# Linear attention in pairs of batches, with 64x64 quarters of the matmul array

## The chip, the cores and the metric

The kernel runs on one core of one Trainium2 chip. The metric is the device time of one execution in microseconds. The core has a matmul engine (PE, with its weight loads shown as PEld), VectorE (DVE), ScalarE (ACT), GpSimd (POOL) and SyncE (SP), which here only issues loads; 16 DMA engines serve all transfers between HBM and the on-chip memory of 128 partitions. Matmul results go to PSUM[...].

## The reference

Two parts follow each other: a linear attention with a norm, and a mixture of experts in which each token goes to one expert.

```python
# q, k, v: (8 batches, 8 heads, 576 tokens, 64) fp32
kv  = einsum('bhsd,bhse->bhde', k, v)        # 64 x 64 per batch and head
out = einsum('bhsd,bhde->bhse', q, kv)
rms = sqrt(mean(out * out, axis=-1) + 1e-6)
x   = (out / rms * g_norm)                   # then (4608 tokens, 512)

logits     = x @ w_gate                      # 8 experts
expert_idx = argmax(logits, axis=1)
gate_w     = softmax(logits)[expert_idx]
for e in range(8):                           # w1: 512 x 1024, w2: 1024 x 512
    ye = relu(x[mask_e] @ w1[e]) @ w2[e]
    out[mask_e] = gate_w * ye
```

## The kernel before

The attention stage works on 36 tiles of 128 tokens with all 8 heads (512 values a token). A batch has 576 tokens, that is four and a half tiles. Of each batch, 512 tokens lie with four tokens in each of 128 partitions; the 64 tokens left over ("rem") of two batches share a tile, 64 partitions each. So a pair of batches has nine tiles: four, four, and one of the remainders.

```python
def load_qkv(src, b):
    t = PA.tile([128, 8, 256], F32, tag="ld", bufs=6, name="ld")
    nc.sync.dma_start(
        t, src[b, :, 0:512, :].rearrange("h (p j) d -> p h (j d)", j=4)
    )
    return t

def load_rem(t, src, b, eng):
    bb = b % 2
    eng.dma_start(
        t[64 * bb:64 * bb + 64, :, :], src[b, :, 512:576, :].transpose([1, 0, 2])
    )
```

One piece of a main load is thus four tokens of one head, 4 x 64 x 4 B = 1 KB, and one of a remainder 256 B. The sums k^T v of a batch are made for two heads at a time, in two column halves of the array:

```python
def kv_mm(b, i):
    # ...
    for j in range(5):
        for hh in range(2):
            h = 2 * i + hh
            if j < 4:
                lhs = kb[:, h, 64 * j:64 * j + 64]
                rhs = vb[:, h, 64 * j:64 * j + 64]
            else:
                lhs = kr[r0:r0 + 64, h, :]
                rhs = vr[r0:r0 + 64, h, :]
            nc.tensor.matmul(
                kvp[64 * hh:64 * hh + 64, i, :], lhs, rhs,
                start=(j == 0), stop=(j == 4),
            )
```

They are copied to a block-diagonal matrix of two heads (`kvs`, zero elsewhere), with 16 more columns that hold kv times the gate's weights. One tile of q is transposed (`x_qt`), copied by ScalarE (`x_qs`) and multiplied with these matrices, 128 rows by 144 columns:

```python
def x_mm(s):
    P, r, b = split(s)
    if r < 8:
        parts = [(slice(0, 128), kvs_bufs[b % 4])]
    else:
        parts = [(slice(0, 64), kvs_bufs[(2 * P) % 4]),
                 (slice(64, 128), kvs_bufs[(2 * P + 1) % 4])]
    op = PSA.tile([128, 2, 512], F32, tag="op", bufs=2, name="op")
    for i in range(4):
        c0 = (i % 2) * 144
        for c, kvs in parts:
            nc.tensor.matmul(
                op[c, i // 2, c0:c0 + 144], qts[s][:, i, c], kvs[:, i, :],
                start=True, stop=True,
            )
    return op
```

`x_norm` squares `op` on ScalarE (`sq`), sums on VectorE (`ms`), makes the factor with ln and exp on ScalarE (`lnt`, `rinv`), and scales on VectorE: the gate's columns (`lr`) and the rows (`xg`). After four or five tiles a `Route` finds the expert of each token and its rank there; GpSimd then writes each tile's rows to a scratch in HBM by an indirect DMA (`xs_scratch`). The order of one step is fixed by hand:

```python
for s in range(36):
    op = x_mm(s)
    for fn in mid[s]: fn()
    if s + 2 < 36: qt = x_qt(s + 2)
    rest = x_norm(s, op)
    if s + 2 < 36: x_qs(s + 2, qt)
    for fn in late[s]: fn()
    rest()
    for fn in last[s]: fn()
```

`load_batch(b + 2)` and the copies `heads` of q (GpSimd, from the loaded tile to one with the heads side by side) are put into `last`, `kv_mm` into `late`. The loads of the first two experts' weights follow those of the last batches in the same queue. Then, in the second stage, each expert's rows are gathered, transposed (`xp`), multiplied by w1 (`hp`), put through relu (`ht`), multiplied by w2 (`yp`), scaled (`ys`) and scattered to the output.

Of the kernel before, what the change touches and what calls it, by code (L numbers as in the profile page):

```python
# [21 lines left out]
def _bc(ap: bass.AP, insert_pos: int, count: int) -> bass.AP:  # L22
    dims = [list(d) for d in ap.ap]
    dims.insert(insert_pos, [0, count])
    return bass.AP(tensor=ap.tensor, offset=ap.offset, ap=dims)
# [3 lines left out]
def kernel(  # L29
# [11 lines left out]
    nc = tc.nc  # L41
# [30 lines left out]
    for P in range(4):  # L72
        for bb in range(2):
            for j in range(4):
                c32[:, o + 9 * P + 4 * bb + j] = (2 * P + bb) * S + 4 * ar + j
        c32[:64, o + 9 * P + 8] = 2 * P * S + 512 + ar[:64]
        c32[64:, o + 9 * P + 8] = (2 * P + 1) * S + 512 + ar[:64]
# [29 lines left out]
    wg = P_const.tile([128, 4, 8], F32, tag="wg")  # L107
    g2 = P_const.tile([128, 1], F32, tag="g2")
    gw = P_const.tile([128, 4, 2, 8], F32, tag="gw")
# [20 lines left out]
    class Weights:  # L130
# [19 lines left out]
        def stage_in(self, pool, tag, bufs):  # L150

            self.s1, self.s2 = [], []
            for dst, src in ((self.s1, moe_w1), (self.s2, moe_w2)):
                rows = src[self.e, :, :].rearrange("o (t p) f -> p (o t) f", p=128)
                n = rows.shape[1] // 2
                for m in range(2):
                    t = pool.tile([128, n, rows.shape[2]], F32, tag=tag, bufs=bufs, name="ws")
                    nc.sync.dma_start(t, rows[:, n * m:n * m + n, :])
                    dst.extend([t[:, kk, :] for kk in range(n)])

        def half1(self, eng, kk):
            if kk == 0:
                self.w1 = P_w.tile([128, 4, F], F16, tag="w1e", bufs=2, name="w1e")
            st = self.s1[kk] if isinstance(self.s1, list) else self.s1[:, kk, :]
            if eng is nc.scalar:
                eng.activation(self.w1[:, kk, :], st, ACTF.Copy, scale=g2)
            else:
                eng.tensor_scalar(  # L168
                    self.w1[:, kk, :], st, g2, 1.0, op0=ALU.mult, op1=ALU.mult,
                )  # L170

        def half2(self, kk):
            if kk == 0:
                self.w2 = P_w.tile([128, 8, D], F16, tag="w2e", bufs=2, name="w2e")
            if isinstance(self.s2, list):
                for m in (2 * kk, 2 * kk + 1):
                    nc.scalar.copy(self.w2[:, m, :], self.s2[m])
            else:
                nc.scalar.copy(  # L179
                    self.w2[:, 2 * kk:2 * kk + 2, :], self.s2[:, 2 * kk:2 * kk + 2, :]  # L180
                )
# [6 lines left out]
    with (  # L188
# [4 lines left out]
        kvs_bufs = []  # L193
        for n in range(4):
            t = PA.tile([128, 4, 144], F32, tag=f"kvs{n}", name=f"kvs{n}")
            kvs_bufs.append(t)

        def load_qkv(src, b):
            t = PA.tile([128, 8, 256], F32, tag="ld", bufs=6, name="ld")
            nc.sync.dma_start(  # L200
                t, src[b, :, 0:512, :].rearrange("h (p j) d -> p h (j d)", j=4)
            )
            return t

        def rem_tile(tag):
            return PA.tile([128, 8, 64], F32, tag=tag, bufs=2, name=tag)

        def load_rem(t, src, b, eng):
            bb = b % 2
            eng.dma_start(  # L210
                t[64 * bb:64 * bb + 64, :, :], src[b, :, 512:576, :].transpose([1, 0, 2])
            )

        ld, rem, qp, kvst = {}, {}, {}, {}
        srcs = {"k": k, "v": v, "q": q}

        def load_first():

            for n in "kvq":
                rem[n, 0] = rem_tile(n + "r")  # L220
                if n != "q":
                    ld[n, 0] = PA.tile([128, 8, 256], F32, tag="ld", bufs=6, name="ld")
            for n, eng in (("k", nc.sync), ("v", nc.scalar)):
                load_rem(rem[n, 0], srcs[n], 0, eng)
                for hs in (slice(0, 4), slice(4, 8)):
                    eng.dma_start(
                        ld[n, 0][:, hs, :],
                        srcs[n][0, hs, 0:512, :].rearrange("h (p j) d -> p h (j d)", j=4),
                    )
            nc.sync.dma_start(cf, c_f32.ap())  # L230
            ld["q", 0] = load_qkv(q, 0)
            nc.scalar.dma_start(wg, moe_w_gate.rearrange("(t p) j -> p t j", p=128))
            nc.scalar.dma_start(g2[0:64, :], g_norm.unsqueeze(1))
            nc.scalar.dma_start(g2[64:128, :], g_norm.unsqueeze(1))
            for n in "kv":
                ld[n, 1] = load_qkv(srcs[n], 1)
                load_rem(rem[n, 0], srcs[n], 1, nc.sync)
            ld["q", 1] = load_qkv(q, 1)
            for b in range(2):
                load_rem(rem["q", 0], q, b, nc.sync)  # L240
            nc.sync.dma_start(ch, c_f16.ap())

        def load_batch(b):
            for n in "kvq":
                ld[n, b] = load_qkv(srcs[n], b)
                if b % 2 == 0:
                    rem[n, b // 2] = rem_tile(n + "r")
                    for bb in range(2):
                        load_rem(rem[n, b // 2], srcs[n], b + bb, nc.sync)

        def heads(b, j):

            if j == 0:
                qp[b] = PA.tile([128, 4, 8, 64], F32, tag="qp", bufs=2, name="qp")
            tv = ld["q", b].rearrange("p h (j d) -> p h j d", j=4)
            nc.gpsimd.tensor_copy(qp[b][:, j, :, :], tv[:, :, j, :])  # L256


        def kv_mm(b, i):
            if i == 0:  # L260
                kvst[b] = PSA.tile([128, 4, 64], F32, tag="kvp", bufs=1, name="kvp")
            kvp = kvst[b]
            kb, vb = ld["k", b], ld["v", b]
            kr, vr = rem["k", b // 2], rem["v", b // 2]
            r0 = 64 * (b % 2)
            for j in range(5):
                for hh in range(2):
                    h = 2 * i + hh
                    if j < 4:
                        lhs = kb[:, h, 64 * j:64 * j + 64]  # L270
                        rhs = vb[:, h, 64 * j:64 * j + 64]
                    else:
                        lhs = kr[r0:r0 + 64, h, :]
                        rhs = vr[r0:r0 + 64, h, :]
                    nc.tensor.matmul(  # L275
                        kvp[64 * hh:64 * hh + 64, i, :], lhs, rhs,
                        start=(j == 0), stop=(j == 4),
                    )

        def kv_copy(b):  # L280
            kvp, kvs = kvst[b], kvs_bufs[b % 4]
            for hh in range(2):
                ps = slice(64 * hh, 64 * hh + 64)
                nc.vector.tensor_copy(kvs[ps, :, 64 * hh:64 * hh + 64], kvp[ps, :, :])

        def kv_t(b):
            kvs = kvs_bufs[b % 4]
            kvtp = PSA.tile([128, 4, 128], F32, tag="misc", bufs=1, name="kvtp")
# [534 lines left out]
```

## Time and profile before

The median of three runs is 307.33 us (306.12 the lowest). The profiled execution has a span of 303.6 us.

| group | count | busy us | mean ns of one |
|---|---|---|---|
| PE `op` = q times kv, 128x144 (and the remainders' form) | 320 records | 45.5 | 301 |
| PE `kvp` = k^T v, 128x64 | 512 records | 22.0 | 228 |
| DVE `ms`, sums of squares | 36 | 24.4 | 679 |
| DVE `xg`, scaled rows | 36 | 24.5 | 681 |
| ACT `sq` / `qts` | 36 / 36 | 21.4 / 20.9 | 593 / 582 |
| POOL scatter to the scratch | 36 | 35.4 | 983 |

The page gives for each engine its busy share in the span and in 40 slices of 7.6 us, in tenths; the rows DMA and GB/s say how busy the 16 DMA engines were and what they moved. A matmul of fp32 shows as two records. Records of the PE overlap in time, so the distance between starts says more than the duration of one. The stages can be told apart by the groups: the first `op` starts at 21.3 us, the last tile's rows are scaled at 131.4 us, and the experts' products run from 145 us to the end. A table of stretches gives busy times, the granted clock of the PE, the DMA share and GB/s for any window.

### The profile page before, as it was taken

To read this page: it belongs to the slowest core of one execution; us is meant where nothing else is said; L and a number is where in the kernel's file an instruction comes from. 1 tells how busy PE (TensorE), PEld (TensorE's weight loads), DVE (VectorE), ACT (ScalarE), POOL (GpSimd) and SP (SyncE) were. 2 spreads that over 40 slices of the span, in tenths; PEclk is the share of its full clock that TensorE was granted. 3 is DMA by queue.
4 is the path that set the end of the run, shared out by engine and by line. 5 is a ranking of instruction groups with operands and counts; after the bars stand their busy time and mean duration, and the time that the engine had idled before them with its cause. 6 is when DMAs were issued, how large, how long until landed. Compare 5 with 4: busy or idle time off the path is not lost.

```text
span 303.6 us, 6229 instructions
## 1 busy us (share of the span) xinstructions
PE 275.5 (91%) x2349; PEld 189.7 (62%) x2349; DVE 164.0 (54%) x431; ACT 159.2 (52%) x342; POOL 153.2 (50%) x205
## 2 busy tenths in 40 slices
PE   8697989899989987647979999999999999999993
PEld 3376877788878886513644756647566574665652
DVE  0024576768778777781237946445464553556140
ACT  1024556556564665488530674737657365672831
POOL 9332016438636764665762576457365663215052
PEclk9799999999999999869999999999999999999998
DMA  6999999999999999922894299979799898968421
GB/s 188 341 284 279 243 279 349 301 276 351 333 299 315 386 401 405 367 105 71 268 364 171 86 367 305 399 220 393 282 346 347 266 388 276 353 279 270 167 101 66
DMA packets 59790, 85.66 MB, mean 282 GB/s; under 512 B 16493, under 2 KB 41326, under 8 KB 59760
## 3 DMA queue, kind: packets, MB, share of 16 engines
q1 hardware_dynamic: 50512, 65.10, 67.7%
q0 software_dynamic: 6976, 18.96, 17.2%
q10 hardware_dynamic: 2272, 1.20, 1.5%
q8 instruction: 19, 0.31, 0.4%
q14 instruction: 11, 0.09, 0.1%
HBM read 71.71 MB, written 15.50 MB: 287 GB/s over the span
## 4 chain that ended last, share of the span: by engine, by line
PE 30%; issue 10%; DMA 9%; POOL 4%; POOLq 1%
PE yp L691 14%; PE hp L677 14%; DMA out_dram<-ys,idx 7%; POOL out_dram L699 2%; DMA xe<-xs_scratch,rowi 2%; PE xp L658 2%; POOL xe L630 2%; POOLq L818 0%; POOL xs_scratch L450 0%; POOLq L699 0%; POOLq L630 0%; POOLq L783 0%
## 5 line engine op out<-in xcount | busy, mean ns | idle before, releaser
L684 ACT ACTIVATE ht<-hp 128x320 f16<-128x320 f32 (+1 forms) x136 | 57.9, 428 | 70.0 <-PE hp L677 58.6
L677 PE MATMUL hp<-xt,w1e 128*128 128x320 f16 (+1 forms) x544 | 79.3, 294 | 0.1
L699 POOL DMA_INDIRECT out_dram<-ys,idx x41 | 42.6, 1038 | 65.7 <-DVE ys L696 56.6
L691 PE MATMUL yp<-w2e,ht 128*128 128x512 f16 x328 | 72.3, 379 | 0.0
L677 PEld LDWEIGHTS <-w1e 128*128 128x128 f16 x544 | 50.3, 98 | 18.8 <-issue 0.6
L696 DVE TENSOR_SCALAR ys<-yp,xe 128x512 f32<-128x512 f32 x41 | 30.6, 750 | 47.2 <-PE yp L691 47.2
L691 PEld LDWEIGHTS <-ht 128*128 128x128 f16 x328 | 32.1, 98 | 37.2
L339 PE MATMUL op<-kvs,qts 128*128 128x144 f32 (+1 forms) x320 | 45.5, 301 | 5.5 <-ACT kvt L292 2.5
L630 POOL DMA_INDIRECT xe<-xs_scratch,rowi x40 | 40.5, 1012 | 14.4 <-issue 10.2
L339 PEld LDWEIGHTS op<-kvs,qts 128*128 128x128 f32 (+1 forms) x320 | 38.1, 184 | 9.0 <-ACT kvt L292 3.1
L450 POOL DMA_INDIRECT xs_scratch<-xg,sli x36 | 35.4, 983 | 13.3 <-issue 10.8
L661 DVE COPY xt<-xp 128x512 f16<-128x512 f16 x41 | 17.4, 425 | 37.2 <-PE xp L658 37.2
L256 POOL COPY qp<-ld 128x512 f32<-128x512 f32 x32 | 18.5, 614 | 32.1 <-DMA ld<-in_q_dram 30.0
L179 ACT CAST w2e<-ws 128x1024 f16<-128x1024 f32 x32 | 31.0, 1042 | 0.0
L359 ACT ACTIVATE sq<-op 128x512 f32<-128x512 f32 x36 | 21.4, 593 | 14.2 <-PE op L339 13.9
L364 DVE TENSOR_REDUCE ms<-sq 128x8 f32<-128x512 f32 x36 | 24.4, 679 | 6.5 <-ACT sq L359 6.4
L326 ACT COPY qts<-qtp 128x512 f32<-128x512 f32 x36 | 20.9, 582 | 7.8 <-PE qtp L321 7.8
L275 PE MATMUL kvp<-ld 128*64 128x64 f32 x512 | 22.0, 228 | 3.4 <-DMA ld<-in_v_dram 3.3
L378 DVE TENSOR_TENSOR xg<-op,rinv 128x512 f16<-128x512 f32 x36 | 24.5, 681 | 0.3
L275 PEld LDWEIGHTS kvp<-ld 128*64 128x64 f32 x512 | 17.7, 137 | 8.5 <-issue 7.5
L368 ACT ACTIVATE lnt<-ms,epsb 128x8 f32<-128x8 f32 x36 | 10.9, 302 | 22.9 <-DVE ms L364 22.8
L168 DVE TENSOR_SCALAR w1e<-ws,g 128x1024 f16<-128x1024 f32 x32 | 22.2, 756 | 0.0
(92 smaller groups left out, 246.7 us busy)
## 6 DMA issues: line engine op xcount, KB each, us to landing
ws<-in_moe_w_dram SPq DMA_DIRECT2D x16, 2048.0 KB, 12.0
ld<-in_q_dram SPq DMA_DIRECT2D x8, 1024.0 KB, 11.1
ld<-in_k_dram SPq DMA_DIRECT2D x7, 1024.0 KB, 8.8
ld<-in_v_dram SPq DMA_DIRECT2D x7, 1024.0 KB, 10.9
ws<-in_moe_w_dram SPq DMA_DIRECT2D x4, 1024.0 KB, 16.8
kr<-in_k_dram SPq DMA_DIRECT2D x8, 128.0 KB, 9.2
ld<-in_k_dram SPq DMA_DIRECT2D x2, 512.0 KB, 7.5
ld<-in_v_dram ACTq DMA_DIRECT2D x2, 512.0 KB, 9.4
```

Of the source, the lines that this page charges most:

```text
L179: nc.scalar.copy(self.w2[:, 2 * kk:2 * kk + 2, :], self.s2[:, 2 * kk:2 * kk + 2, :])
L275: nc.tensor.matmul(kvp[64 * hh:64 * hh + 64, i, :], lhs, rhs, start=(j == 0), stop=(j == 4),)
L339: nc.tensor.matmul(op[c, i // 2, c0:c0 + 144], qts[s][:, i, c], kvs[:, i, :], start=True, stop=True,)
L364: nc.vector.reduce_sum(ms, sq, axis=AXX)
L378: nc.vector.tensor_tensor(xg[:, r, 0:512].rearrange("p (c i h n) -> p c i h n", c=2, i=2, h=2), ox, _bc(r4, 4, 64), op=ALU.mult,)
L450: nc.gpsimd.indirect_dma_start(out=xs_views[9 * self.P + self.g0 + t], out_offset=IndirectOffsetOnAxis(ap=self.sli[:, t:t + 1], axis=0), i ...
L630: nc.gpsimd.indirect_dma_start(out=xe.bitcast(I32), out_offset=None, in_=xs.ap(), in_offset=IndirectOffsetOnAxis(ap=rows, axis=0), bounds_ ...
L677: nc.tensor.matmul(hp, self.w.w1[:, kk, f * 128:(f + 1) * 128], self.xt[:, kk, ws * wd:(ws + 1) * wd], start=(kk == 0), stop=(kk == 3),)
L684: nc.scalar.activation(self.ht[:, f, ws * wd:(ws + 1) * wd], hp, ACTF.Relu)
L691: nc.tensor.matmul(yp, self.ht[:, f, t * 128:(t + 1) * 128], self.w.w2[:, f, :], start=(f == 0), stop=(f == 7),)
L696: nc.vector.tensor_scalar(ys, yp, self.xe[t][:, 514:516].bitcast(F32), None, op0=ALU.mult)
L699: nc.gpsimd.indirect_dma_start(out=self.views[t], out_offset=IndirectOffsetOnAxis(ap=self.idx[:, t:t + 1], axis=0), in_=ys, in_offset=None ...
```

## The change

A pair of batches is now one unit. Each batch of a pair has 64 of the 128 partitions, with eight tokens in each and one more from the remainder. All nine tiles of a pair have the same form: rows 0 to 63 from the first batch, 64 to 127 from the second. The purpose is to have every product of k^T v and of q fit a quarter of the array, 64 rows by 64 columns, so that four of them can run side by side and none multiplies the zeros of the block-diagonal matrix.

```diff
-        def load_qkv(src, b):
-            t = PA.tile([128, 8, 256], F32, tag="ld", bufs=6, name="ld")
-            nc.sync.dma_start(
-                t, src[b, :, 0:512, :].rearrange("h (p j) d -> p h (j d)", j=4)
-            )
+        def load_main(n, P, hs, js, eng):
+            for bb in range(2):
+                rows = srcs[n][2 * P + bb, hs, 0:512, :].rearrange("h (p j) d -> p h j d", j=8)
+                dst = main[n, P][64 * bb:64 * bb + 64, hs, :].rearrange(
+                    "p h (j d) -> p h j d", d=64
+                )
+                eng.dma_start(
+                    dst[:, :, js, :].rearrange("p h j d -> p h (j d)"),
+                    rows[:, :, js, :].rearrange("p h j d -> p h (j d)"),
+                )
 ... (k and v are loaded in two halves of heads; the first and last q in two halves of tokens)
+        def kv_mm(P, i):
+            for j in range(9):
                 for hh in range(2):
                     h = 2 * i + hh
+                    for bb in range(2):
+                        ps = slice(64 * bb, 64 * bb + 64)
+                        ... (lhs, rhs: rows ps of k and v, 64 columns; j == 0 is the remainder)
+                        nc.tensor.matmul(
+                            kvst[P][64 * hh:64 * hh + 64, bb, 64 * i:64 * i + 64], lhs, rhs,
+                            start=(j == 0), stop=(j == 8),
+                        )
 ... (kv of both batches is copied by one ScalarE copy in place of two VectorE copies a batch)
         def x_mm(s):
             op = PSA.tile([128, 2, 512], F32, tag="op", bufs=2, name="op")
+            kvs = kvsb[s // 9]
             for i in range(4):
+                c0 = 256 * (i // 2) + 72 * (i % 2)
+                for c in range(2):
+                    for r in range(2):
+                        rs, cs = slice(64 * r, 64 * r + 64), slice(64 * c, 64 * c + 64)
+                        n0 = 72 * (i % 2)
+                        nc.tensor.matmul(
+                            op[cs, r, c0:c0 + 72], qts[s][rs, i, cs],
+                            kvs[rs, c, i // 2, n0:n0 + 72], start=True, stop=True,
+                        )
```

A piece of a main load is now eight tokens of a head, 2 KB (1 KB where the tokens are halved), and each load is two transfers, one to partitions 0 to 63 and one to 64 to 127. Remainders stay pieces of 256 B. A head has 64 columns and 8 columns of the gate, so the tile's products are 16 of 64 x 64 by 72 columns in place of 4 of 128 x 128 by 144.

Other parts move with it. `kvp` takes two PSUM banks, and `qtp` has one buffer in place of two. The main tiles of q lie in the memory of the converted weights and those of k and v of odd pairs in that of the weights' loads, so the first expert's weights are loaded to the memory of k and v of even pairs, and the second's after `kv_mm` of the last pair. The loads are asked for earlier: k and v of the next pair but one as soon as their memory is free. `heads` copies one tile at a time, four tiles ahead. In the first three pairs the routing is cut in smaller pieces one to four steps later, where VectorE waits for ScalarE:

```diff
-            at(last, s, rt.first)
-            at(mid, s + 2, rt.ranks)
-            at(late, s + 2, rt.send)
+            if P < 3:
+                at(late, s + 1, rt.first_a)
+                at(late, s + 2, rt.first_b)
+                at(mid, s + 3, rt.ranks)
+                at(late, s + 4, rt.send)
 ...
-        at(last, 21, W[0].stage1)
-        at(last, 21, W[0].stage2)
-        at(last, 30, W[1].stage_in, PA, "ld", 6)
+        at(last, 17, W[0].stage_in, PA, ("kA", "vA"))
+        at(last, 26, W[1].stage1)
+        at(last, 26, W[1].stage2)
```

The experts' stage is the same but for where the weights come from.

## The prediction, made before the changed kernel was run

> **What bounds the kernel now.** I read, in this order, the busy shares and the slices of the page, a table of stretches, the PE's timeline in the middle of the attention, and a table of three stretches of the DMA queue. The page first:
>
> ```profile
> PE 275.5 (91%) x2349; PEld 189.7 (62%) x2349; DVE 164.0 (54%) x431; ACT 159.2 (52%) x342; POOL 153.2 (50%) x205
> PE   8697989899989987647979999999999999999993
> DMA  6999999999999999922894299979799898968421
> GB/s 188 341 284 279 243 279 349 301 276 351 333 299 315 386 401 405 367 105 71 268 364 171 86 367 305 399 220 393 282 346 347 266 388 276 353 279 270 167 101 66
> ```
>
> Two stages with different limits. A slice is 7.6 us. In the first 17 slices (the attention, with the first two experts' weights behind it) both the PE row and the DMA row stand at 9; then comes the hand-over to the experts; from 158 us on the PE alone is full. The stretches give numbers to that:
>
> ```profile
> 2.00:21.30 19.30, 16.59 (x137) 8.96 (x134) 1.67 (x6) 1.18 (x3) 10.77 (x23) 0.91 1.08 302
> 21.30:44.00 22.70, 19.23 (x242) 16.91 (x241) 12.87 (x36) 12.06 (x31) 2.26 (x4) 1.00 1.12 261
> 44.00:131.40 87.40, 76.31 (x906) 67.38 (x903) 66.48 (x196) 48.56 (x129) 50.59 (x87) 0.98 1.05 337
> 158.00:303.60 145.60, 140.85 (x935) 84.74 (x932) 72.91 (x157) 77.70 (x149) 69.28 (x68) 0.99 0.76 269
> ```
>
> The columns are length, busy time of PE, PEld, DVE, ACT and POOL, granted clock, DMA share, GB/s. The attention tiles run from 21.3 to 131.4 us, 110 us for 36 tiles, 3.06 us each. The DMA share is 1 all the way. The bytes add up: 302 x 19.3 + 261 x 22.7 + 337 x 87.4 = 41.2 MB, which is q, k and v (28.3 MB), two experts' weights (8.4) and the scattered rows (36 x 128 x 1032 B = 4.8). So in the attention stage the DMA queue has about as much to do as the PE: it has nearly no slack. Within the tiles:
>
> ```profile
> 44.03 1.25 PE L339 MATMUL op<-kvs,qts 128*128 128x144 f32 x8
> 45.19 0.66 PE L321 MATMUL qtp<-cf,qp 128*128 128x128 f32 x4
> 45.78 0.69 PE L275 MATMUL kvp<-ld 128*64 128x64 f32 x16
> 46.39 0.33 PE L275 MATMUL kvp<-vr,kr 64*64 64x64 f32 x4
> 46.66 1.20 PE L339 MATMUL op<-kvs,qts 128*64 128x144 f32 x16
> 47.79 0.66 PE L290 MATMUL kvtp<-cf,kvs 128*128 128x128 f32 x4
> ```
>
> Read starts against starts, because the durations overlap. An fp32 matmul is two records (four matmuls of a tile show as x8). The products of q over the full array take 45.19 - 44.03 = 1.16 us for 8 records, 145 ns a record; the tile with remainders does 16 records with half the columns in 1.13 us, 71 ns a record. So two column tiles really run side by side. k^T v does 16 records in 0.61 us (38 ns each). Last, how the queue moves:
>
> ```profile
> 41.00:43.00 2.00, 2.00 (x31) 1.76 (x30) 1.88 (x8) 1.50 (x4) 0.00 (x0) 1.00 1.15 191
> 70.00:80.00 10.00, 9.86 (x125) 8.61 (x124) 8.12 (x20) 6.21 (x15) 7.72 (x14) 1.00 1.08 361
> 105.00:125.00 20.00, 16.66 (x163) 15.04 (x160) 15.05 (x48) 10.79 (x30) 10.69 (x19) 0.91 1.03 402
> ```
>
> With the share at 1 in all three, 191 GB/s is where remainders (64 partitions, 256 B pieces) are loaded, 361 mostly 1 KB pieces over 128 partitions, 402 mostly weights (2 and 4 KB pieces over 128 partitions).
>
> [...] the only 64-partition loads here run at 191 GB/s, but their pieces are also small, so the two causes can't be told apart. [...] The timeline above shows two tiles running together; four at once no line here shows.
>
> **The change part by part.** *PE.* q times kv becomes 16 matmuls of 64x64 by 72 columns in place of 4 of 128x128 by 144. Four at a time this is 4 rounds x 2 records of about 65 ns (half of 145, less what is fixed): 0.55 us against 1.16, so -0.6 us a tile. If the records were bound by their number at the 38 ns seen in k^T v, it would be 32 x 38 = 1.2 us and nothing gained; I take 0.7. k^T v goes from 640 records (32 steps of 0.88 us = 28 us) to 1152. In fours at some 70 ns a round they take 20 us, at 25 ns each 29 us. Transposes of q stay at 0.6 us a tile[...]. Sum: 0.7 + 0.6 + 0.3 + 0.7 (k^T v) + 0.15 (transposed kv, gate) = 2.45 us a tile, from about 2.95 once the kernel runs evenly.
> *DVE and ACT.* The row of sums takes 679 ns, the gate product 223, the normalized rows 681: 1.58 us, plus routing of about 2.8 us per 4.5 tiles = 0.6, plus the wait for ln and exp between them (0.61 us, partly filled now because the routing is cut into pieces placed there). That gives 2.3 to 2.4 us a tile. ACT stays at 1.7. qtp goes from two buffers to one, which the order of the tile hides. So the engines would allow about 2.4 us a tile: 36 x 2.4 + 3 us at pair boundaries = 90 us.
> *Start.* The first tile needs both batches of k and v (4.7 MB) in place of one (2.4) before its kv exists. At the 341 GB/s of the second slice that is 7 us more, of which the present order (q and the next k load in that time) takes some back: tiles start at about 26 us, against 21.3.
> *DMA.* The same 28.3 MB. The main pieces grow from 1 to 2 KB, which at 128 partitions should go at 370 to 390 GB/s. But every main load is now two transfers of 64 partitions, one per batch, one behind the other in the same queue. Remainders: 3.1 MB at the 191 GB/s or less of the stretch above, 16 to 22 us, as before. Main loads: 25.2 MB. [...] All of q, k and v is then in at 2 + 20 + 68 + 4 (scattered rows) = 94 us, or at 2 + 20 + 117 + 4 = 143 us. The last pair's nine tiles can't start before its q is in.
> *Weights.* Two experts, 8.4 MB at 400 GB/s, 21 us behind q. The experts' stage itself is not touched.
>
> **How it can go.**
> Main case[...]: the first half of the last q lands at about 136 us, its first tile runs at 139, nine tiles of 2.35 us and 2.5 us of tail end at 162-163, against 132. The weights are in at about 164, before they are needed (hand-over plus 10 us). The whole moves by +30: 307.3 + 30 = 337 us.
> Rival 1, the halves overlap[...]: then the DMA is ahead, the engines set the end at 26 + 90 + 2 = 118, and the weights land by 94 + 21 + some scattered rows = 118. The whole moves by -13.5: 294 us. For it: the 2 KB pieces, and PE near full in the stretch from 44 us[...].
> Rival 2, partial overlap, main loads at 260 GB/s: 97 us, last q at 123, its nine tiles end at about 145: +13, 320 us.
> Rival 3, the PE doesn't run four tiles at once: 1.2 us a tile for q and 44 us for k^T v make 3.3 us a tile, 26 + 36 x 3.3 = 145: again +13 or more, whatever the DMA does. Two at a time are shown, so I give this 10%.
>
> **Range and chances.** [...] partial overlap or a slow PE 15%, full overlap 30%. The middle of that, pulled a little from the main case, is 329 us. Eight times in ten it should lie between 290 and 346: the low end is rival 1 with a good tile rate[...]. Faster by over 2% (below 301): 0.31. Within 2%: 0.08. Slower (above 313.5): 0.61.
>
> **What would show it.** If the main case is right: the GB/s row stands near 200 to 230 until all of q is in, with the DMA share still at 1; PE and DVE rows fall below 9 in the attention stage; waits of qp, the PE's kvp and qtp on DMA of q, k and v become the longest; in the weights' stretch it is back at 400. If rival 1 is right, the row is at 350 or more from the third slice on and no DMA wait is long. The PE part is right if the starts of the op groups lie 0.55 to 0.8 us before the next group, wrong if 1.1 or more. The start is right if the first op is at 25 to 32 us. The stretch from the last tile to the end should be unchanged (172 us). What would break the prediction: halves that overlap in the queue, or attention tiles that take over 2.7 us with their data there.

## The result, and the profile after

The changed kernel takes 358.78 us (median of 4 runs, 357.99 to 359.31) against 306.73 us before on the same chip (median of 4, one of them 459.21): 1.171 times as long, 95% interval 1.166 to 1.175. The profiled execution has a span of 355.7 us. The page's rows, in slices of 8.9 us:

```profile
PE 271.1 (76%) x3684; PEld 180.5 (51%) x3684; DVE 157.0 (44%) x411; ACT 159.0 (45%) x338; POOL 152.7 (43%) x206
PE   7088725486653963676636999999999999999994
DMA  7998999999999999994122792799798989896712
GB/s 150 223 218 185 200 228 226 214 210 249 254 217 221 258 246 293 377 381 169 67 99 74 254 361 81 274 308 398 237 400 260 363 284 383 262 394 202 282 61 83
```

The DMA row stands at 8 or 9 from the second to the 18th slice, nearly as before, but up to the 15th (133 us) it now moves 185 to 258 GB/s in place of some 300. The PE row falls, mostly to between 3 and 7, in the attention stage; from slice 23 on (196 us) it is full again. The table of stretches (length; busy PE, PEld, DVE, ACT, POOL; granted clock; DMA share; GB/s):

```profile
2.00:37.00 35.00, 22.38 (x391) 14.07 (x388) 0.90 (x4) 2.36 (x5) 8.69 (x19) 0.80 1.02 206
37.00:139.00 102.00, 58.66 (x1599) 48.34 (x1599) 46.85 (x128) 39.91 (x105) 32.61 (x59) 0.81 1.07 231
139.00:162.00 23.00, 15.84 (x397) 13.23 (x398) 9.34 (x26) 9.38 (x24) 8.11 (x15) 0.73 1.02 378
200.00:355.00 155.00, 149.97 (x1015) 91.21 (x1013) 76.42 (x169) 83.75 (x163) 77.47 (x76) 0.99 0.78 277
```

Until 139 us q, k and v come in at 206 to 231 GB/s with the DMA share at 1: the median packet of 2 KB takes 156 ns in the trace. The weights behind them, over all 128 partitions, come at 378. The last piece of q, k and v lands at 140.9 us (105.7 before). But that is not all, because the last pair of batches doesn't start then. The PE's timeline at four places:

```profile
39.81 0.73 PE L361 MATMUL op<-kvs,qts 64*64 64x72 f32 x32 [0.68 <-DVE xg L400]
40.47 0.66 PE L345 MATMUL qtp<-cf,qp 128*128 128x128 f32 x4
...
56.46 1.11 PE L292 MATMUL kvp<-vB,kB 64*64 64x64 f32 x64
57.39 0.30 PE L361 MATMUL op<-kvs,qts 64*64 64x72 f32 x6
61.93 0.71 PE L361 MATMUL op<-kvs,qts 64*64 64x72 f32 x26 [4.23 <-issue]
...
65.72 0.68 PE L361 MATMUL op<-kvs,qts 64*64 64x72 f32 x20
71.07 0.75 PE L361 MATMUL op<-kvs,qts 64*64 64x72 f32 x12 [4.67 <-issue]
...
149.01 0.54 PE L361 MATMUL op<-kvs,qts 64*64 64x72 f32 x18
152.97 0.47 PE L361 MATMUL op<-kvs,qts 64*64 64x72 f32 x14 [3.42 <-issue]
153.37 0.66 PE L309 MATMUL kvtp<-cf,kvs 128*128 128x128 f32 x4
...
156.06 1.24 PE L361 MATMUL op<-kvs,qts 64*64 64x72 f32 x32 [0.32 <-DVE kvs L323]
```

The first two lines: the 32 records of a tile's products of q take 40.47 - 39.81 = 0.66 us, so four quarters do run side by side. The next: a group of products that belong together is torn apart, 6 records before a gap of over 4 us and 26 after it; the next one 20 and 12. In the gap the PE waits for nothing that the trace names ("issue"). Count weight loads and matmuls between the end of one such gap and the start of the next: 254. Between 57.7 and 153.0 us there are ten such gaps of 1.3 to 5.4 us, 34.0 us in all; seven of them follow the one before after 254 or 255 instructions, the others later. The page has the cause in another place, the queue of the instruction stream (number of transfers, MB, share), after and before:

```profile
q8 instruction: 29, 0.48, 0.6%
q8 instruction: 19, 0.31, 0.4%
```

Each transfer is 16 KB (16384 B in both traces). With a weight load to each matmul record the changed kernel has 2 x 3684 = 7368 PE instructions, 28.8 times 256, and 29 transfers; the kernel before has 2 x 2349 = 4698, 18.4 times 256, and 19. The other kernels below agree: 25 transfers with 3108 or 3181 records, 34 with 4333. So I count a block as 256 instructions, an estimate from these counts and the 254 or 255 of the gaps. And each of the ten gaps ends 1.3 to 1.6 us after the end of such a transfer: those that start at 59.2, 68.2, 129.5, 137.8, 144.0 and 150.5 us end at 60.6, 69.6, 130.8, 139.2, 145.1 and 151.5, and the PE goes on at 61.9, 71.1, 132.2, 140.5, 146.6 and 153.0. The whole list of the PE's waits begins with these (us in total, times, longest):

```profile
PE op L361 <- issue: 18.7, 5, 5.1
PE kvp L292 <- issue: 15.8, 6, 5.4
```

From 30 us on they are 34.0 us; the kernel before has neither wait there. The first product of the last pair is at 156.06 us, 15 us after the last of its q has landed. Only 4.9 us of these 15 are stops; in the rest the PE works off the third pair's last tiles and the last k^T v, which the earlier stops had put back. The last rows are scaled at 182.7 us (132.1 before), and from there to the end it is 173.0 us (171.5 before). All but 1.5 us of the loss lies in the attention stage.

### The profile page after: what moved, and what is told of

It is laid out like the page before. It is cut to its first block, busy times and chain, and to the rows that moved or that the text cites. A ratio compares the mean times of both kernels' runs of the same rounds, so it can differ in the third digit from the quotient of the medians.

```text
span 355.7 us, 8916 instructions
## 1 busy us (share of the span) xinstructions
PE 271.1 (76%) x3684; PEld 180.5 (51%) x3684; DVE 157.0 (44%) x411; ACT 159.0 (45%) x338; POOL 152.7 (43%) x206
## 5 line engine op out<-in xcount | busy, mean ns | idle before, releaser
L705 PE MATMUL hp<-xt,we 128*128 128x320 f16 (+1 forms) x544 | 79.8, 295 | 0.0
L719 PE MATMUL yp<-we,ht 128*128 128x512 f16 x328 | 72.3, 379 | 0.0
L705 PEld LDWEIGHTS <-we 128*128 128x128 f16 x544 | 50.6, 98 | 19.1 <-issue 0.6
L361 PE MATMUL op<-kvs,qts 64*64 64x72 f32 x1152 | 34.8, 264 | 29.1 <-issue 18.7
L275 POOL COPY qp<-qm 128x512 f32<-128x512 f32 x32 | 19.0, 614 | 70.5 <-DMA qm<-in_q_dram 70.5
L361 PEld LDWEIGHTS op<-kvs,qts 64*64 64x64 f32 x1152 | 28.7, 165 | 35.4 <-issue 20.6
L175 ACT CAST we<-ws 128x1024 f16<-128x1024 f32 x32 | 31.0, 1042 | 0.0
L292 PE MATMUL kvp<-vA,kA 64*64 64x64 f32 x512 | 14.0, 268 | 16.3 <-DMA vA<-in_v_dram 8.9
L292 PE MATMUL kvp<-vB,kB 64*64 64x64 f32 x512 | 13.4, 263 | 15.3 <-issue 8.4
L345 PE MATMUL qtp<-cf,qp 128*128 128x128 f32 x128 | 23.7, 314 | 1.0 <-ACT qts L350 0.4
L170 DVE TENSOR_SCALAR we<-ws,g 128x1024 f16<-128x1024 f32 x32 | 22.2, 757 | 0.0
```

Of the source, the lines that this page charges most:

```text
L175: nc.scalar.copy(self.w2[:, 2 * kk:2 * kk + 2, :], self.s2[:, 2 * kk:2 * kk + 2, :])
L292: nc.tensor.matmul(kvst[P][64 * hh:64 * hh + 64, bb, 64 * i:64 * i + 64], lhs, rhs, start=(j == 0), stop=(j == 8),)
L361: nc.tensor.matmul(op[cs, r, c0:c0 + 72], qts[s][rs, i, cs], kvs[rs, c, i // 2, n0:n0 + 72], start=True, stop=True,)
L705: nc.tensor.matmul(hp, self.w.w1[:, kk, f * 128:(f + 1) * 128], self.xt[:, kk, ws * wd:(ws + 1) * wd], start=(kk == 0), stop=(kk == 3),)
L719: nc.tensor.matmul(yp, self.ht[:, f, t * 128:(t + 1) * 128], self.w.w2[:, f, :], start=(f == 0), stop=(f == 7),)
```

## The experiments

The theories. A: one transfer to 64 partitions goes at half the rate, and the two halves of a load, one behind the other in one queue, don't overlap. C: the PE's instructions come in blocks of 256 among the other DMA transfers; while the DMA engines are full of queued loads, blocks are many microseconds apart (4 to 10 from 59.2 to 144.0 us in the trace above), and a kernel with more, smaller matmuls runs out of instructions. Rivals have letters of their own in the expectations.

The chips of these groups are slower than the first: the kernel before takes 332.2, 333.4, 332.6 and 333.1 us in the four groups, against 306.7. Its profile there has 198.5 us in place of 175.9 from the last square (`sq`) to the end, and 134.6 in place of 127.6 up to it. So ratios are compared, and each group has its own runs of the kernel before. Times inside the attention stage, from one profile each ("PE stops": waits of `op` and `kvp` with "issue" from 30 us on):

| kernel | ratio to before | 95% interval | q, k, v landed | `sq` of tile 27 | last `sq` | PE stops |
|---|---|---|---|---|---|---|
| before (on such a chip) | 1 | | 106.5 | 110.5 | 134.6 | 0 |
| changed (on such a chip) | 1.165 | 1.157 to 1.174 | 140.5 | 156.3 | 183.1 | 30.2 |
| before_halves | 1.090 | 1.083 to 1.096 | 137.9 | 130.4 | 159.6 | 0 |
| after_nine | 1.041 | 1.035 to 1.046 | 83.2 | 118.8 | 146.3 | 13.9 |
| nine_spread | 1.034 | 1.026 to 1.041 | 85.7 | 118.1 | 145.8 | 17.0 |
| nine_block | 1.017 | 1.011 to 1.023 | 81.9 | 110.4 | 134.9 | 5.1 |
| after_early | 1.166 | 1.157 to 1.175 | 141.8 | 160.8 | 187.7 | 31.5 |
| after_block | 1.131 | 1.121 to 1.141 | 139.9 | 152.2 | 173.1 | 13.1 |
| block_early | 1.147 | 1.134 to 1.160 | 140.3 | 157.3 | 178.8 | 14.9 |
| after_twoq | 1.198 | 1.186 to 1.210 | 148.0 | 171.2 | 198.0 | 12.6 |
| after_fine | 1.206 | 1.197 to 1.216 | 173.7 | 173.3 | 200.2 | 7.9 |
| before_split16 | 1.029 | 1.018 to 1.040 | 107.1 | 115.0 | 142.2 | 5.1 |

(Tile 27 is the first of the last pair. The 154.5 us that some expectations give for it on the first chip is the square of tile 26; tile 27's is 157.4.)

**The loads alone, in the kernel before.**

```diff
-            nc.sync.dma_start(
-                t, src[b, :, 0:512, :].rearrange("h (p j) d -> p h (j d)", j=4)
-            )
+            rows = src[b, :, 0:512, :].rearrange("h (p j) d -> p h (j d)", j=4)
+            for c in (slice(0, 64), slice(64, 128)):
+                nc.sync.dma_start(t[c, :, :], rows[c, :, :])
```

> The kernel before, with nothing changed but that each main load of q, k and v is two transfers, to partitions 0 to 63 and 64 to 127, in the same queue (the same 1 KB pieces, the same products). Theory A (a transfer to 64 partitions gets half the rate): the GB/s row stands at 200 to 230 until all of q is in at about 140 us, where it was 260 to 370; the time rises by 25 to 45 us. Theory B (the slow loads of the changed kernel come from something else, such as 2 KB pieces or the order of the queue): under 5 us more.

362.22 us against 332.17, 30 us more. Its page's GB/s row (slices of 9 us):

```profile
GB/s 214 223 202 196 204 207 223 275 217 237 248 246 231 250 280 360 402 356 91 109 383 169 34 84 311 222 398 178 403 215 352 222 275 378 175 404 196 217 94 48
```

Same bytes, same order, same products: with the loads cut by halves the row stands at 196 to 275 until the last q is in at 137.9 us, 31 us later. A packet of 1 KB takes 80 ns in place of 47 (medians from 45 to 80 us). The PE has no "issue" stops. Theory A holds, and with it the size of the main case of the prediction, that of slow loads to 64 partitions (+30). The changed kernel loses 52 and 54 us in its two comparisons, so some 22 are from elsewhere.

**The same products, with loads over 128 partitions.** Rows 0 to 63 and 64 to 127 become the even and the odd heads of one batch, nine tokens a row; a load spans 128 partitions in pieces of 2304 B and there are no remainders. The products stay in quarters.

```diff
-                rows = srcs[n][2 * P + bb, hs, 0:512, :].rearrange("h (p j) d -> p h j d", j=8)
+                rows = srcs[n][2 * P + bb].rearrange(
+                    "(g hh) (p j) d -> (hh p) g (j d)", hh=2, j=9)
```

> The changed kernel with the same quarters of the array, but partitions 0 to 63 and 64 to 127 hold an even and an odd head of one batch, nine tokens a row, so that each load is one transfer to all 128 partitions in pieces of 2304 B and there are no remainders. Theory A[...]: GB/s 350 to 390, all of q in at about 80 us, tiles of 2.3 to 2.5 us, time 285 to 300 us. Theory C (besides, the PE stops for several us after every 256 of its instructions, because its instruction stream is fetched through the same full DMA queues): the loads are as fast, but stops of 2 to 5 us stay as long as the queue is full, and the time is 300 to 325 us.

346.05 us, 1.041. The expected times were meant for the first chip; there the ratio makes some 319 us, inside the 300 to 325 of theory C and above the 285 to 300 of A. GB/s of its page, and two gaps of its PE:

```profile
GB/s 290 372 280 397 390 390 390 398 377 184 274 295 52 256 328 33 108 64 66 294 345 2 61 172 254 302 332 289 400 192 383 188 334 315 258 384 202 182 119 31
```

```profile
42.21 0.30 PE L348 MATMUL op<-kvs,qts 64*64 64x72 f32 x8
44.42 0.61 PE L348 MATMUL op<-kvs,qts 64*64 64x72 f32 x24 [1.92 <-issue]
...
48.11 0.69 PE L348 MATMUL op<-kvs,qts 64*64 64x72 f32 x22
50.81 0.46 PE L348 MATMUL op<-kvs,qts 64*64 64x72 f32 x10 [2.01 <-issue]
```

At 390 GB/s all of q is in by 83 us, 23 us earlier than in the kernel before, and still it is slower than that one. The gaps after 254 instructions are there as long as the queue is full, beginning at 42.5, 48.8, 73.8 and 80.1 us; after that the longest is 1.0 us. So the slow loads to 64 partitions (206 to 231 GB/s) are not the cause of the stops.

**The changed kernel with less in the queue, and with less to multiply.** In after_noload the last two pairs take the data of the first two again: their loads are left out, and the output isn't the attention of these batches. In after_kvhalf k^T v of the last three pairs leaves out four of nine tokens. Each ran once.

```diff
+            if P > 1:                                   # after_noload
+                main[n, P], rem[n, P] = main[n, P - 2], rem[n, P - 2]
+                return
...
-            for j in range(9):                          # after_kvhalf
+            js = range(9) if P == 0 else (0, 1, 2, 3, 8)
+            for j in js:
```

> The changed kernel without the loads of the last two pairs: their k, v and q are those of the first two pairs again (that part of the input is left out, all work on the engines stays). From about 75 us on the DMA queue is nearly empty until the weights are loaded. Theory A (only late data holds the tiles up): tiles of the last two pairs run at about 2.3 us and without waits on loads, except where the weights are loaded if theory C holds. Theory C (instruction fetch behind a full queue): the stops after 256 PE instructions are under 1 us while the queue is empty. If the stops stay at 3 to 5 us with an empty queue, the fetch is slow by itself.

> The changed kernel with only five of the nine tokens of each row in the k^T v of the last three pairs (4 of 9 products are left out, all loads stay): 768 PE matmul records and as many weight loads fewer. The products left out are worth about 12 x 0.45 us of PE time. Theory A: the end moves by the end of the loads alone, so it stays within 5 us of the changed kernel. Theory C: the stops after 256 instructions become fewer and shorter, and the time falls by 8 to 20 us.

after_noload: 359.79 us, against 332.17 before. Its PE's timeline where the loads end (the last piece lands at 72.3 us):

```profile
66.92 0.93 PE L368 MATMUL op<-kvs,qts 64*64 64x72 f32 x20
71.92 0.74 PE L368 MATMUL op<-kvs,qts 64*64 64x72 f32 x12 [4.07 <-issue]
72.80 1.12 PE L352 MATMUL qtp<-cf,qp 128*128 128x128 f32 x4
73.84 0.49 PE L299 MATMUL kvp<-vr,kr 64*64 64x64 f32 x8
74.12 1.93 PE L299 MATMUL kvp<-vB,kB 64*64 64x64 f32 x64
75.82 1.18 PE L368 MATMUL op<-kvs,qts 64*64 64x72 f32 x32
```

The last long stop ends as the queue runs dry. After it the same mix of instructions runs on: from 72 to 155 us no "issue" gap of the PE is longer than 0.6 us, as theory C expected (under 1 us), and blocks follow each other within 3.5 us (116.6, 120.1, 123.6, 127.1). In the changed kernel's full queue they follow at 8.3 us (121.1, 129.5, 137.8). This is the clearest sign for the fetch behind the loads. The total fell less than the loads left out would suggest: the late tiles still take 2.9 us each (squares of tiles 18 to 34) where theory A had 2.3, and the start is as late as in the changed kernel.

after_kvhalf: 379.4 us (the changed kernel 387.6 in another group, where the kernel before takes 1.2 us more). PE stops 11.3 us in place of 30.2, `sq` of tile 27 at 151.2 in place of 156.3. Fewer instructions, less waiting, but less work too, so this alone doesn't settle it.

**Changed kernel again, two queues, and an earlier k^T v.** after_again is the changed kernel.

> The changed kernel as it is, on the same chip as the three others of this group, so that their times can be read against it. A ratio to the kernel before of 1.15 to 1.18 as in the first comparison, last square of the last tile about 50 us later than before.

387.56 against 333.37 us: 1.165. The first result repeats on another chip.

```diff
+                eng = (eng, nc.scalar)[bb]              # after_twoq
                 eng.dma_start(
```

> Only change to the changed kernel: the transfers of the second batch of each pair (partitions 64 to 127) are asked for by ScalarE's queue, those of the first batch stay in SyncE's. Theory A ([...] one queue serves one half after the other): both halves are then written side by side, the GB/s row rises from about 220 to 320 or more, all q is in by 80 to 105 us instead of 138, and the time falls by 20 to 40 us against the changed kernel. Rival (the transfer rate is not a matter of which half is written at one time, but of the number or order of the pieces): the row stays near 220 and the time within 5 us of the changed kernel's. PE stops after 256 instructions (theory C) stay as long as the queues are full, in either case.

The time went the wrong way, 1.198, but the stretches settle the dispute about the halves (columns as above):

```profile
51.00:54.00 3.00, 1.21 (x5) 0.66 (x3) 0.00 (x0) 0.00 (x0) 0.61 (x1) 0.50 1.04 365
60.00:63.00 3.00, 0.00 (x0) 0.00 (x0) 0.00 (x0) 0.00 (x0) 0.00 (x0) 0.50 1.09 227
78.00:81.00 3.00, 2.09 (x47) 1.54 (x48) 2.39 (x6) 2.66 (x6) 1.22 (x2) 0.99 1.05 369
84.00:87.00 3.00, 1.26 (x61) 1.00 (x59) 2.91 (x8) 1.46 (x4) 0.00 (x0) 1.00 1.09 217
```

At 51 and 78 us both queues carry 2 KB pieces, one to the low, the other to the high half: 365 and 369 GB/s, 91 to 93 ns a packet (means). At 60 and 84 us only one of them does (the other brings remainders or nothing): 227 and 217 GB/s, 153 and 164 ns. So halves in two queues do overlap. The gain was lost by my edit: ScalarE's queue got both halves of the first v as well, and ScalarE, which has to ask for its loads in the order of its program, came to copy the first k^T v at 47.5 us (a wait of 45.5 us) and its transpose at 71.9 (one of 23.8). The first square came at 75.8 us in place of 36.5. From there to the last square it took 122.2 us, against 146.6 in after_again: the overlap gained 24 us, the late start cost 39.

```diff
-                at(late, f - 5 + i, kv_mm, P, i)        # after_early
+                at(late, f - (9 if P == 3 else 5) + i, kv_mm, P, i)
```

> Only change to the changed kernel: the four steps of k^T v of the last pair are placed four tiles earlier (tiles 18 to 21 instead of 22 to 25), where the PE has time left; everything else as it is. Theory C (the PE's instruction stream, refilled 256 instructions at a time behind the full DMA queue, delays k^T v of the last pair beyond the landing of its q): the last pair's first tile then starts at 139 to 144 us on the scale of the first chip instead of 154.5, and the time falls by 10 to 17 us. Rival D (the stops only move, since as many blocks have to be fetched before the last tile): less than 4 us gained.

No gain, 1.166: rival D. Tile 27's square comes at 160.8, and the PE's stops are 31.5 us (30.2 in after_again); they now fall mostly on the products of q (24.4 us on `op`, 7.1 on `kvp`, in place of 14.9 and 15.3). It isn't one step that is late: moving instructions forward brings none of them to the PE faster.

**The nine-token variant with k^T v over eight tiles.** Each step of the last two pairs is cut in two (`range(5)`, `range(5, 9)`).

> The variant with nine tokens a row and loads over 128 partitions (after_nine, 1.04 times the kernel before on its chip), with each step of k^T v of the last two pairs cut into two halves, spread over eight tiles instead of four. Theory C: the bursts of 216 PE instructions a tile fall to 140, the stops of 2 to 3 us at 73 to 82 us go, and 4 to 10 us are gained: 0.99 to 1.03 times the kernel before. Rival E (with the data there, the chain ScalarE - VectorE - PE and the PE's lower granted clock set the tile's time, not its instructions): within 3 us of 1.04 times the kernel before.

1.034, an interval that overlaps that of 1.041: theory C's 4 to 10 us didn't come, and the stops stay (17.0 us in place of 13.9). As with rival D above, the number of instructions is the same and the stops only move.

**Half the instructions for q.** kv is put into a block-diagonal matrix again, and a tile's products of q are 8 of 128 rows in place of 16 of 64 (32 PE instructions in place of 64). More PE work: 1.13 us a tile in place of 0.66.

```diff
-                    for r in range(2):
-                        nc.tensor.matmul(op[cs, r, c0:c0 + 72], qts[s][rs, i, cs],
-                            kvs[rs, c, i // 2, n0:n0 + 72], start=True, stop=True)
+                    nc.tensor.matmul(
+                        op[cs, i // 2, 256 * (i % 2):256 * (i % 2) + 144],
+                        qts[s][:, i, cs], kvs[:, 2 * c + i // 2, i % 2, :],
+                        start=True, stop=True)
```

> The kernel before as it is, for a profile on the chip of this group. Last square of the last tile at 126 to 134 us and about 200 us from there to the end, if the 25 us by which this kind of chip is slower than the first lie in the experts' stage, as in all variants here; an attention stage 20 us longer if they lie there.

> The changed kernel with its loads, but the products of q take 128 rows by 64 columns with a block-diagonal kv (8 matmuls of 144 columns a tile in place of 16 of 72): 32 PE instructions a tile for them in place of 64, and more PE work, some 1.15 us a tile in place of 0.66. Theory C (in a full queue the PE gets 256 instructions about every 8 us, and that sets when the last pair begins): 27 tiles x 32 = 864 instructions less before the last pair, 3.4 blocks, so its first tile starts at 140 to 145 us, where its q lands, in place of 154 to 157, and the time falls by 8 to 16 us against the changed kernel. Rival F (the PE's own work is what counts): 36 x 0.5 us more, slower by 5 to 18 us.

> The variant with nine tokens a row and loads over 128 partitions, with k^T v spread over eight tiles (nine_spread, 1.03 times the kernel before), and now the products of q as 8 of 128 rows by 64 columns with a block-diagonal kv, 32 PE instructions a tile in place of 64. Theory C: fewer stops until the queue is empty at 80 us, tile 15 reached 4 to 8 us earlier, 0.99 to 1.02 times the kernel before. Rival E (the chain over ScalarE, VectorE and PE sets the tile's time): within 3 us of nine_spread. Rival F (PE work counts): slower than nine_spread by over 4 us.

> The changed kernel with each main load cut into one transfer for each head and batch (128 KB instead of 512 KB or 1 MB), so that transfers to the low and the high 64 partitions alternate four to eight times as often in the one queue. Theory A (one queue serves one half after the other): packets stay at about 150 ns, the GB/s row at 200 to 230, the time within 6 us of the changed kernel's. Rival (short transfers overlap at their ends, and both halves are written together): packets of 2 KB below 125 ns, the row above 260, the last q in before 125 us, and 10 us or more gained.

before_again: 335.3 us, one execution. Its profile is 29.6 us longer than the first chip's, 7.0 in the attention and 22.6 in the experts' stage, so the first alternative, nearly.

after_block: 376.62 us, 1.131 against 1.165, about 11 us gained by products that cost the PE more. nine_block: 1.017 against 1.034, about 5.5 us gained; tile 15's square at 73.3 us in place of 78.5. PE waits of the two:

```profile
PE op L369 <- issue: 7.4, 3, 3.4
PE kvp L292 <- issue: 6.7, 7, 2.9
```

```profile
PE op L356 <- issue: 3.3, 4, 2.2
PE kvp L276 <- issue: 3.0, 3, 1.3
```

The gains are those of theory C in both, and rival F holds in neither. But tile 27 of after_block starts at 150.9 us (its square at 152.2), not at 140 to 145: a miss. nine_block has most of both causes taken away, and its attention ends where that of the kernel before does (134.9 and 134.6). It doesn't beat it, although its loads are in 25 us earlier: from 84 to 130 us the PE is busy for 38.6 of 46 us and VectorE for 35.2, and the PE's longest waits there are for VectorE (3.4 us of `op` for `xg`, 1.8 of `pp` for `oh`). Which of the two sets the pace was not tested.

after_fine, short transfers that alternate between the halves: 1.206, a loss. A packet of 2 KB falls to 107 to 110 ns in the mean, as the rival said, but the rest of the rival's forecast fails, because the DMA engines don't stay full (share 0.57 to 0.72 between 50 and 80 us, 169 to 212 GB/s): SyncE asks for 44 transfers of 128 KB in these 30 us, about one in 0.7 us. With the engines less than full, the stops are 7.9 us in place of 30.2.

**The number of instructions alone, in the kernel before.** The products of q are cut into 64 columns by 72 or by 36.

```diff
-                for c, kvs in parts:
-                    nc.tensor.matmul(op[c, i // 2, c0:c0 + 144], qts[s][:, i, c], kvs[:, i, :], ...)
+                for n in range(0, 144, 72):             # 36 in before_split32
+                    for c, kvs in parts:                # c: two halves of 64 columns
+                        nc.tensor.matmul(op[c, i // 2, c0 + n:c0 + n + 72], qts[s][:, i, c],
+                            kvs[:, i, n:n + 72], ...)
```

> The kernel before with its loads; only the products of q are cut in 16 matmuls of 64 columns by 72 in place of 4 of 128 by 144 (same multiplications, two column tiles side by side, 64 PE instructions a tile in place of 16, 113 in all in place of 65). Theory C (the PE gets 256 instructions every 6 to 8 us while the queue is full): one block lasts 2.3 tiles, 6.9 us at 3.06 us a tile, so stops begin to show, 0 to 12 us lost. Rival (the count doesn't matter): the PE's work is about the same, within 4 us of the kernel before.

> As the run before, but 32 matmuls of 64 columns by 36: 128 PE instructions a tile for the products of q, 177 in all. Theory C: 36 x 177 / 256 = 25 blocks, each 6 to 8 us while the queue is full, so stops of 1 to 4 us after every 256 instructions, and 20 to 50 us lost. Rival (the count doesn't matter, only the PE's own time): 64 records at the 38 ns of k^T v over two column tiles are 1.2 us a tile against 1.16, so less than 6 us lost, and no gap that returns after 256 instructions.

> The changed kernel with the block-diagonal products of q (after_block, 1.13 times the kernel before), and the four steps of k^T v of the last pair four tiles earlier. Theory G (with fewer instructions to fetch, these steps, 15 us of PE order between the landing of q and the last pair, are what is left): its first tile starts at 140 to 147 us in place of 152, and 4 to 10 us are gained, 1.10 to 1.12. Rival D (as in after_early, the stops only move): within 3 us of after_block.

before_split16: 341.93 against 333.14 us. A tile's products take 1.15 us in place of 1.08 where nothing stops them, 2.5 us for all 36; stops that the kernel before doesn't have make up 5.1 us:

```profile
67.18 1.10 PE L340 MATMUL op<-kvs,qts 128*64 128x72 f32 x28
69.94 0.35 PE L340 MATMUL op<-kvs,qts 128*64 128x72 f32 x4 [1.66 <-issue]
...
75.28 0.78 PE L340 MATMUL op<-kvs,qts 128*64 128x72 f32 x17
76.63 0.72 PE L340 MATMUL op<-kvs,qts 128*64 128x72 f32 x15 [0.57 <-issue]
```

Same loads, same multiplications, more instructions: 8.8 us lost (interval 6 to 13), more than the rival's 4 and in the middle of theory C's 0 to 12. before_split32 tells less: 377.68 us (1.130), but a tile's 64 records take 2.16 us, 34 ns each. The expectation of 1.2 us had halved the 38 ns of k^T v, which already came with two column tiles side by side. So the PE itself is slower, and the loss can't be parted between that and the fetch. (The profiled execution took 395.41 us, at a mean granted clock of 0.87; the 2.16 us is the median of its groups.) It is inconclusive for C.

block_early: 1.147 against 1.131 on another chip, intervals that overlap: no gain. Tile 26's square came at 149.9, with k^T v of the last pair done, and at 149.1 in after_block, so rival D fits up to there. Then the PE stood still until 155.03 us, but not for instructions: it waited 4.36 us for GpSimd's copy of kv to the block-diagonal matrix (`kvb`), which stood behind a wait of 5.04 us of GpSimd's own. That copy is part of the block-diagonal variant, so this run doesn't show cleanly what the earlier k^T v is worth.

**A rule that fits the runs roughly.** A pair of the changed kernel has 9 x 72 instructions for q, 576 for k^T v and some 70 others: 5.1 blocks of 256. From 59.2 to 144.0 us eleven blocks came, 7.7 us each, so 39 us a pair, 4.3 us a tile; measured from tile 9 to tile 27, on the first chip: 4.3. With nine tokens blocks come every 6.4 us in the full queue (41.9, 48.4, 54.8, 61.1): 3.6 a tile; measured over the first 15 tiles 3.35. nine_block has 3.9 blocks a pair: 2.8 a tile, measured 3.0. The kernel before, in as full a queue, needs a block only every 11.0 us (from 19.7 to 107.8 us), which is slower than the 6.4 to 7.7 us at which they came in the variants: it has no stops.

## Why the prediction was wrong

*The loads to 64 partitions:* right in effect and size, but the 117 us for the main loads rested on a rate that no trace of before showed (the 68 us beside them are 25.2 MB at 370 GB/s, an estimate between the 361 and the 402 of the stretches). 206 to 231 GB/s were moved; the last q was to be in at 143 us and its first half at about 136, and they landed at 140.9 and 133.6. before_halves shows it alone: 30 us.

*The PE's products:* right. 0.7 us a tile predicted, 0.66 measured; k^T v takes 57.39 - 56.46 = 0.93 us for 64 records, 15 ns each, better than the 20 us in all that I had put at the low end. Rival 3 is out. The 0.3 us in the sum for a tile was my estimate; no trace shows it.

*The step that failed:* "its first tile runs at 139" once the first half of q has landed at 136. It ran at 156.06. The sum of the main case, 337 us, is off by 21.8: 17.1 from this step, 3.1 from nine tiles that took 26.6 us to the last scaled rows in place of 23.5, 1.6 from the rest. One of the prediction's own signs of being wrong came true: these nine tiles, with their data there, took 2.96 us each, over the 2.7 named. What I hadn't on my list: the PE's own instructions are a load too, in the same full DMA engines, and the change raises its matmul records from 2349 to 3684. I counted the records for their duration only, and took the DMA wait to be the one wait that could end last. The page before has the clue, a small instruction queue among the DMA queues, which I passed over. In the changed kernel the stops had come to 34.0 us by then. after_noload shows them gone with the queue empty, before_split16 shows the higher count at work with the loads as they were, after_block and nine_block show a part of it undone.

*The start:* wrong by its size. First product at 36.2 us, where I said 26. I used 341 GB/s for the loads of the first pair and the lower rate for the rest in the same main case; at 206 GB/s the 4.7 MB of k and v alone take 23 us, and they had landed at 26.2 us. Another 10 us, for which the 26 left no room, went to the last k^T v (to 31.5 us) and the copies and transposes between it and the first product. The last q still came no later than foreseen.

*The stretch to the end:* right, 173.0 us for 172.

*Rivals 1 and 2, and the range:* the main case had 55%, and the pull from 337 to 329 came from chances for overlapping halves. In one queue the row shows no such overlap (206 to 231 GB/s). The upper end of 346 left room for slower loads only, and none for a wait that I didn't know.

*A reading of before:* the PE row of the 17 slices was said to stand at 9; it reads 6 to 9. Nothing in the sum rests on it.

*Lower clock:* the prediction took full speed. The granted clock was 0.81 from 37 to 139 us. After the gap of 3.4 us that ends at 153.0 us, 0.51 was granted from 154.7 to 161.6 us, and the group of `op` at 156.06 us took 1.24 us in place of 0.73. Why the clock fell was not shown, and what share of the 3.1 us this is was not measured apart.

What stays open: what makes up the 11 us by which the first product of tile 27 of after_block (150.9 us) is behind its q; how much of the 22 us beyond the loads comes from the number of instructions (halving those for q gave back 11); and whether a balanced pair of queues would make the changed layout as fast as loads over 128 partitions, which wasn't tried.

## What to carry to other kernels

Cutting a matmul into quarters multiplies instructions, and while the DMA engines were full of queued loads the PE here got only 256 of them every 6 to 8 us: count PE instructions per microsecond beside their busy time, and look for gaps that return after 256. Lay data out so that one transfer spans 128 partitions (390 GB/s in after_nine; two transfers to 64 in one queue moved 206 to 231 in the changed kernel); if it can't, two queues at once are worth a try, on engines that aren't needed for other work: the rate is shown here (365 to 369 GB/s), a faster kernel is not. When a wait ends in "issue" in the middle of a group of products, look at the number of instructions first: moving work to earlier tiles gained nothing clear in any of three runs here, halving the instructions for q gained 11 and 5.5 us.

## What the runs showed of the hardware

- Two 64-partition transfers to different halves, in two queues: 365 to 369 GB/s; one half alone: 217 to 227 (after_twoq). In one queue, one behind the other, two such transfers moved 206 to 231 GB/s.
- Instruction blocks of 16 KB: 1.0 to 1.4 us each for the transfer itself (changed kernel, 59.2 to 150.5 us), 7.7 us apart on average with the loads at 206 to 231 GB/s, 6.4 with loads at 390, and 3.5 without a stop when the queue is empty. In the changed kernel's profile a stop of the PE ends 1.3 to 1.6 us after the transfer has.
- Distance of fp32 matmul records: 15 to 21 ns in four quarters, 34 to 36 ns in two column tiles of 128 x 64, whether 72 or 36 columns are streamed (before_split16 and before_split32).
